# GpSimd's additions and reciprocal root moved in their steps, and PSUM additions given to VectorE in the second batch

## The chip, the cores and the metric

One core of one Trainium2 chip runs the whole program. The metric is device microseconds (us) of one execution, the median of several runs. A profiled execution is one further run, recorded by the hardware profiler; its engines are called PE (TensorE, with PEld for its weight loads), DVE (VectorE), ACT (ScalarE), POOL (GpSimd) and SP (the queue that issues most DMAs).

## What is computed

Inputs are q, k, v of shape (8 batches, 8 heads, 576 positions, 64) and two MLP weights, all float32. First comes attention in which each row keeps its 32 largest scores:

```python
scores = scale * np.matmul(q, k.transpose(0, 1, 3, 2))
kth = np.partition(scores, -top_k, axis=-1)[..., -top_k:-top_k + 1]
scores = np.where(scores >= kth, scores, -1000000000.0)
attn = np.exp(scores - np.max(scores, axis=-1, keepdims=True))
attn = attn / (np.sum(attn, axis=-1, keepdims=True) + 1e-09)
x = np.matmul(attn, v)          # heads side by side: x is (8, 576, 512)
```

Then Fourier mixing over positions and channels, a normalisation, and an MLP of width 2048:

```python
mixed = np.real(np.fft.fft(np.fft.fft(x, axis=1), axis=2))
u = x + mixed
un = (u - mean(u)) / np.sqrt(var(u) + 1e-06)      # over the 512 channels
out = u + np.maximum(un @ w_ch1, 0.0) @ w_ch2
```

## The kernel before

The attention is cut into 288 tiles of 128 query rows (36 to a batch). One pass of the main loop is a *step*: in step i VectorE searches the 32 largest scores of tile i (second half) and tile i+1 (first half). It is four rounds of MAX8 and three of MATCH_REPLACE8 on 128x576 scores (L446, L448, in `top_ops`). TensorE makes the scores of tile i+3 (`scores`, L392 to L425), into one of six score buffers S. After the search GpSimd forms the tile's bounds nt (L455, `bounds`), ScalarE the mask (L469), GpSimd subtracts it (L472), ScalarE takes the exponential (L480) and splits the words (L493); a DMA writes them to DRAM ("planes") and another brings them back transposed (PT), and TensorE multiplies by v a few steps later (L585, o). The result is transposed back (L626, tpx), and VectorE normalises it into the batch's x (L630). Two x buffers exist, so a batch writes its x only when the batch two before it has stored its own.

Behind the attention of a batch follow its Fourier section and its MLP, laid between the steps of the next batch's attention. The Fourier section: GpSimd folds x into sums and differences (L685, L696, L762, near), TensorE transforms along positions (L809, yp), ScalarE copies that out (L834 to L847, y and yt), TensorE transforms along channels (L860, L864, mp; `dft_channels`), and the result is added to x. Only row tiles 0, 1 and 4 are computed; tiles 3 and 2 get the mirrored channels of tiles 0 and 1. There are two ways to add it:

- `add_mixed` (batches 1 to 6; batches count from 0): ScalarE copies mp from PSUM to a tile us (L874), GpSimd adds it to x (L898), a step later VectorE takes the statistics.
- `add_at_once` (first and last batch): VectorE adds from PSUM directly (L880): four additions for tile 0 and its mirror, four for tile 1, one for tile 4, nine in all.

Then `stats` (L909, L910, VectorE) per row tile, `rsqrt` (variance to reciprocal root: three VectorE operations, then four Newton passes of four GpSimd operations each, L928 to L933), and `channels_first` (x transposed on TensorE, L948, and copied out by ScalarE, L951, unT). The MLP is a queue of *units*: 32 hidden units a batch (L1055, hp, relu on ScalarE, L1059), then units of the second product. That second product is plain for the first batch (`back`, L1082) and for the last two row tiles of batches 1 to 5, and in seven half-size products elsewhere (L1254, cv and cw). In `back`, ScalarE scales the finished product (L1108) and GpSimd adds it to x (L1110); for row tile 3, VectorE does both (L1096), a step later.

The order of the work is written by the program itself: `at(step, where, fn)` files a piece of work under a step and a place in it; `run(i, where)` plays it back. Units are taken from the queue between the fixed pieces of a step so that the TensorE cost per step, counted with fixed numbers (1.75 us for a unit of the second product), stays level until the next batch's units arrive (`arrivals`, `level`). All engines execute in that order. Places on GpSimd, in order within a step: mask subtraction, whatever the units issue, "pool0", sums for the seven products, the bounds nt, then "pool" and "pool2". On VectorE: search, late work, "dve", "stats". Stores are filed under "load2", last in the step, on SP's or GpSimd's queue.

Matmul results of this part go to three PSUM banks used in turn (`bank`). A bank may be held until its reader has been issued.

In the second batch (`soon`, b = 1), step 81 holds the channel transforms of row tiles 0 and 1, step 82 that of tile 4, steps 81 to 83 the additions, 82 to 84 the statistics, 84 the root, and its MLP units arrive at step 86.

Of the kernel before, what the change touches and what calls it, by code (L numbers as in the profile page):

```python
# [86 lines left out]
def kernel(  # L87
# [761 lines left out]
    def dft_channels(b, t, quick=False):  # L849

        rows, y = ROWS[t], y_of[b]
        shape, name = [P, 2, DM // 2], f"mp_{b}_{t}"
        mp = ps_s.tile(shape, F32, name=name, tag="sp") if b == B - 1 else bank(shape, name)
        def of(g):
            if t == 4:
                return yt_of[b][:, g].rearrange("p h r -> p (h r)")
            return y[:, g, t, :]

        for g in range(2):
            nc.tensor.matmul(  # L860
                mp[0:rows, 0, g:DM // 2:2], lhsT=of(g), rhs=fd[:, g], start=True, stop=True
            )
        for g in range(2, 4):
            nc.tensor.matmul(  # L864
                mp[0:rows, 1], lhsT=of(g), rhs=fd[:, 2 * g - 2:2 * g],
                start=(g == 2), stop=(g == 3),
            )
        if quick:
            at(now[0], "dve", lambda: add_at_once(b, t, mp))
            return 1.75  # L870
        if b not in us_of:
            us_of[b] = batp.tile([P, 3, DM], F32, name=f"us_{b}", tag="fold_s")
        us = us_of[b][0:rows, CHUNKS[0].index(t), :]
        nc.scalar.copy(out=two(us), in_=mp[0:rows])  # L874
        return 1.75
# [36 lines left out]
    def rsqrt(b):  # L912

        vr = small.tile([P, 5], F32, name=f"vr_{b}", tag="vr", bufs=2)
        gi = small.tile([P, 5], I32, name=f"gi_{b}", tag="gi", bufs=2)
        t2 = small.tile([P, 5], F32, name=f"t2_{b}", tag="t2", bufs=2)
        rs_of[b] = rs = gi.bitcast(F32)
        nc.vector.tensor_scalar(
            out=vr, in0=mv[b % 2][:, :, 1], scalar1=1e-6, scalar2=None, op0=ALU.add
        )  # L920
        nc.vector.tensor_scalar(
            out=gi, in0=vr.bitcast(I32), scalar1=1, scalar2=None, op0=ALU.arith_shift_right
        )
        nc.vector.tensor_scalar(
            out=gi, in0=gi, scalar1=-1, scalar2=0x5F3759DF, op0=ALU.mult, op1=ALU.add
        )
        for _ in range(4):
            nc.gpsimd.tensor_tensor(out=t2, in0=rs, in1=rs, op=ALU.mult)  # L928
            nc.gpsimd.tensor_tensor(out=t2, in0=t2, in1=vr, op=ALU.mult)
            nc.gpsimd.tensor_scalar(  # L930
                out=t2, in0=t2, scalar1=-0.5, scalar2=1.5, op0=ALU.mult, op1=ALU.add
            )
            nc.gpsimd.tensor_tensor(out=rs, in0=rs, in1=t2, op=ALU.mult)  # L933

    def channels_first(b, t):

# [104 lines left out]
    def mlp_units(b):  # L1041
# [33 lines left out]
        def back(ch, t, part):  # L1075
            n, hT, rs = CHUNKS[ch].index(t), hT_of[ch], rs_of[b]
            if part == 0:
                cps[t] = bank([P, DM], f"cp_{b}_{t}", True)
            cp, free = cps[t]
            if t != 4:  # L1080
                for it in range(2 * part, 2 * part + 2):
                    nc.tensor.matmul(  # L1082
                        cp, lhsT=hT[:, it, P * n:P * (n + 1)], rhs=w2[:, it, :],
                        start=(it == 0), stop=(it == NIT - 1),
                    )
                if part == 7:
                    xt = x[:, t, :]

                    def store():
                        store_rows(b, t)  # L1090
                        stored.append(t)
                        if len(stored) == 4:
                            written.add(b)

                    def finish():
                        nc.vector.scalar_tensor_tensor(  # L1096
                            out=xt, in0=cp, scalar=rs[:, t:t + 1], in1=xt, op0=ALU.mult, op1=ALU.add
                        )
                        free()

                    if last:
                        finish()
                    elif t == 3:

                        late_next.append(finish)
                    else:
                        ct = ct_of(t)
                        nc.scalar.mul(out=ct, in_=cp, mul=rs[:, t:t + 1])  # L1108
                        free()
                        nc.gpsimd.tensor_tensor(out=xt, in0=xt, in1=ct, op=ALU.add)  # L1110

                    if last:
                        store()
                    else:
                        at(now[0] + 2 + t % 2, "load2", store)
                return

            for it in range(2 * part, 2 * part + 2):
                for g in range(2):
                    nc.tensor.matmul(  # L1120
                        cp[TAIL * g:TAIL * (g + 1), :],
                        lhsT=hT[:, NIT // 2 * g + it, P * n:P * n + TAIL],
                        rhs=w2[:, NIT // 2 * g + it, :],
                        start=(it == 0), stop=(it == NIT // 2 - 1),
                    )
            if part == 3:
                tails_done(cp, free)
                if begins:
                    begins.pop()()
# [269 lines left out]
    def at(step, where, fn, cost=0.0):  # L1399
        plan.setdefault((step, where), []).append(fn)  # L1400
        costs[step] = costs.get(step, 0.0) + cost
# [92 lines left out]
    for b in range(B):  # L1494
        end = PER_BATCH * (b + 1) - 1
        last = b == B - 1
        first, soon = b == 0, b == 1
        T0 = end + (2 if first else 3 if soon or last else 5)
        for hp in range(NPB - 1):
            at((end - 4 + (0, 2, 3)[hp] if first else end + hp), "pool2", lambda b=b, hp=hp: fold_pair(b, nc.gpsimd, hp))  # L1500
        quick = first or last
        for n, op in enumerate(fold_tails(b, nc.gpsimd)):
            if quick:
                at(T0 - 2 if first else T0 - 1, "pool" if first else "pool0", op)
            else:
                at(T0 + n - (2 if soon else 1), "pool0", op)

        def folds(b=b, T0=T0, quick=quick, soon=soon, last=last):
            ops = fold_ops(b, nc.vector if quick else nc.gpsimd)
            for n, op in enumerate(ops):  # L1510
                if quick:
                    op()
                    if last and n == 0:
                        some_sums(1.3)
                else:
                    at(T0 + 1 + (min(n, 3) if soon else n), "pool0", op)

        at(T0, "dve" if quick else "begin", folds)
        if last:

            at(T0 + 1, "pe1", lambda: one_unit() + one_unit() if len(queue) > 1 else 0.0)
        ft, fc = {
            "first": ((T0 + 1, T0 + 1), T0 + 1), "last": ((T0 + 1, T0 + 2), T0 + 3),
            "soon": ((T0 + 6, T0 + 7), T0 + 7), "": ((T0 + 6, T0 + 8), T0 + 9),
        }["first" if first else "last" if last else "soon" if soon else ""]
        if first:
            at(ft[0], "pe1", lambda b=b: dft_tokens_both(b), 5.8)
        else:
            for par in range(2):
                at(ft[par], "pe1", lambda b=b, par=par: dft_tokens(b, par), 2.9)  # L1530
        for n, t in enumerate((0, 1, 4)):
            s = fc + (0 if quick else n // 2)
            at(s, "pe2", lambda b=b, t=t, q=quick: dft_channels(b, t, q), 1.75)
        for n, t in enumerate((0, 1, 4, 3, 2)):
            s = fc + (n // 3 if last else 0 if first else (0, 0, 1, 1, 2)[n])
            if quick:
                at(fc, "stats", lambda b=b, t=t: stats(b, t))
            else:
                at(s, "pool2", lambda b=b, t=t: add_mixed(b, t))
                at(s + 1, "dve", lambda b=b, t=t: stats(b, t))  # L1540
            at(s + (1 if quick else 2), "pe", lambda b=b, t=t: channels_first(b, t), 0.6)
            if first and t == 4:
                at(s + 1, "pe", lambda: (queue.extend(waiting), waiting.clear()) and 0.0)
        at(s + 1, "begin" if quick else "dve", lambda b=b: rsqrt(b))
        arrivals.append(s + (1 if quick else 3))
        at(arrivals[-1], "units", lambda b=b: (queue if b else waiting).extend(mlp_units(b)))

    queue, waiting, pending, written, now, out_next = [], [], [], set(), [0], []
# [261 lines left out]
```

## Time and profile before

| what | value |
|---|---|
| median of 3 runs | 1774.47 us (1772.94 to 1776.26) |
| profiled execution, its own time | 1769.09 us |
| its span, first to last instruction | 1767.3 us |
| busy: TensorE / VectorE / ScalarE / GpSimd | 92% / 88% / 72% / 51% of the span |
| mean granted TensorE clock | 0.968 of full |

A row of the timeline gives start, duration, engine, line, operation, output and input, and how many instructions were merged; in square brackets stands the idle time before it and what ended it. The columns of the stretches are busy time and instruction count of each engine, then TensorE's granted clock, the DMA engines' busy share and GB/s. In the groups of instructions the numbers behind the bar are busy time, mean ns of one, and idle time of the engine just before, with what ended most of it. A row of the waits gives the total, how many, and the longest.

### The profile page before, as it was taken

Reading aid. Unit: us, or ns where it says so; the run is one execution under the profiler, and the core shown is the slowest. Engines: PE = TensorE matmul, PEld = TensorE weight load, DVE = VectorE, ACT = ScalarE, POOL = GpSimd, SP = SyncE. Lnnn points to the kernel's source line nnn. Section 1 sums busy time; section 2 is a strip of 40 time slices with the busy share of each in tenths; the row PEclk is TensorE's granted clock in tenths of the full one; section 3 lists DMA queues with packets and bytes.
Section 4 is the critical chain, followed back from the end, with each engine's and each line's share of the span. In section 5 each row is a group of like instructions: output and inputs, shape, how many; then the busy total and the mean of one; then the engine's idle time right before and its main releaser. Section 6 shows DMA issues by size and latency. Waiting matters only on the chain.

```text
span 1767.3 us, 26298 instructions
## 1 busy us (share of the span) xinstructions
PE 1631.0 (92%) x7830; PEld 1044.8 (59%) x7830; DVE 1548.3 (88%) x3319; ACT 1278.2 (72%) x3136; POOL 907.0 (51%) x1269
## 2 busy tenths in 40 slices
PE   5666789999899999999999999999999999999999
PEld 2444455464465755666556755576566755678777
DVE  7999999999999999999899999999999999873121
ACT  6887769886888778877888778777877778653200
POOL 4667876656636465455544565366535555433000
PEclk8878889999999999999999999999999999999999
DMA  5333226661457855596557846585558645643151
GB/s 157 103 92 95 78 82 173 184 156 41 127 139 198 223 134 137 142 235 167 130 140 185 230 125 147 148 239 152 142 133 223 183 128 132 171 126 102 36 182 60
DMA packets 492926, 255.28 MB, mean 144 GB/s; under 512 B 364528, under 2 KB 483056, under 8 KB 492784
## 3 DMA queue, kind: packets, MB, share of 16 engines
q1 hardware_dynamic: 489008, 243.80, 52.0%
q0 software_dynamic: 2816, 9.44, 1.6%
q8 instruction: 63, 1.03, 0.2%
q14 instruction: 79, 0.65, 0.1%
q10 hardware_dynamic: 960, 0.36, 0.1%
HBM read 99.79 MB, written 84.74 MB: 104 GB/s over the span
## 4 chain that ended last, share of the span: by engine, by line
PE 51%; DVE 17%; ACT 15%; POOL 10%; issue 4%; DMA 2%; SPq 0%; POOLq 0%; DVEq 0%; ACTq 0%
PE hp L1055 20%; DVE m L446 8%; DVE wk L448 8%; PE o L585 7%; PE cw L1254 5%; PE cv L1254 4%; PE sp L422 4%; POOL wk L472 4%; ACT wk L469 3%; PE cp L1120 3%; POOL fold L696 3%; ACT S L425 2%; ACT wk L493 2%; PE tpP L548 1%; PE sp_t L392 1%
## 5 line engine op out<-in xcount | busy, mean ns | idle before, releaser
L472 POOL TENSOR_TENSOR wk<-S,wk 128x576 f32<-128x576 f32 x288 | 407.4, 1415 | 444.9 <-ACT wk L469 444.0
L446 DVE MAX8 m<-wk 128x8 f32<-128x576 f32 x864 | 618.2, 742 | 0.1
L1055 PE MATMUL hp<-unT,w 128*128 128x256 f32 (+1 forms) x2048 | 528.5, 409 | 11.0 <-ACT hT L1059 3.7
L1055 PEld LDWEIGHTS hp<-unT,w 128*128 128x128 f32 x2048 | 377.3, 191 | 116.9 <-ACT hT L1059 10.4
L448 DVE MATCH_REPLACE8 wk<-m,wk 128x576 f32<-128x576 f32 x576 | 425.6, 739 | 0.0
L493 ACT COPY wk<-S 128x576 uint16<-128x576 uint16 x468 | 290.7, 675 | 0.0
L469 ACT ACTIVATE wk<-S,nt 128x576 f32<-128x576 f32 x288 | 224.8, 780 | 89.5 <-POOL nt L455 88.7
L446 DVE MAX8 m<-S 128x8 f32<-128x576 f32 x288 | 214.9, 746 | 11.2 <-ACT S L396 10.5
L480 ACT ACTIVATE S<-wk,nt 128x576 f32<-128x576 f32 x234 | 185.5, 793 | 46.5 <-POOL wk L472 45.6
L448 DVE MATCH_REPLACE8 wk<-m,S 128x576 f32<-128x576 f32 x288 | 212.8, 739 | 0.3 <-issue 0.3
L1059 ACT ACTIVATE hT<-hp 128x320 f32<-128x320 f32 (+1 forms) x256 | 104.6, 413 | 140.2 <-PE hp L1055 135.1
L1082 PE MATMUL cp<-w,hT 128*128 128x512 f32 x448 | 205.5, 597 | 0.0
L585 PE MATMUL o<-PT,v 128*64 128x256 f32 (+3 forms) x1440 | 196.5, 417 | 6.3 <-DMA PT<-planes 3.9
L422 PE MATMUL sp<-kT,qT 64*128 64x512 f32 (+1 forms) x528 | 163.2, 660 | 7.1 <-ACT S L414 4.2
L585 PEld LDWEIGHTS o<-PT,v 128*64 128x64 f32 x1440 | 114.4, 154 | 82.1 <-issue 21.6
L425 ACT COPY S<-sp 128x512 f32<-128x512 f32 (+1 forms) x264 | 141.9, 590 | 28.3 <-PE sp L422 27.3
L455 POOL TENSOR_TENSOR nt<-m,cc 128x2 f32<-128x2 f32 x288 | 57.5, 200 | 167.5 <-DVE m L446 162.2
L1254 PE MATMUL cw<-w,hT 128*128 128x256 f32 x512 | 120.3, 385 | 7.5 <-ACT ct L1225 2.8
L1082 PEld LDWEIGHTS cp<-w,hT 128*128 128x128 f32 x448 | 80.7, 192 | 76.4 <-issue 76.0
L392 PEld LDWEIGHTS sp_t<-kt,qT 128*128 128x128 f32 x320 | 50.1, 192 | 107.3 <-issue 63.9
L1254 PEld LDWEIGHTS cw<-w,hT 128*128 128x128 f32 x512 | 96.2, 192 | 24.3 <-POOL hT L1198 4.2
L1254 PE MATMUL cv<-w,hT 128*128 128x256 f32 x432 | 99.4, 380 | 0.0
(156 smaller groups left out, 2038.9 us busy)
## 6 DMA issues: line engine op xcount, KB each, us to landing
planes<-wk SPq DMA_DIRECT2D x208, 288.0 KB, 2.6
w<-w_parts SPq DMA_DIRECT2D x94, 512.0 KB, 4.7
space<-in_moe_w_ch_dram SPq DMA_DIRECT2D x32, 512.0 KB, 3.4
nat<-in_q_dram SPq DMA_DIRECT2D x128, 64.0 KB, 2.3
v<-in_v_dram SPq DMA_DIRECT2D x32, 256.0 KB, 3.4
nat<-in_k_dram SPq DMA_DIRECT2D x62, 128.0 KB, 2.8
planes<-wk SPq DMA_DIRECT2D x52, 144.0 KB, 2.6
w_parts<-w_t POOLq DMA_DIRECT2D x8, 512.0 KB, 4.5
```

The lines of the kernel that those rows point to most:

```text
L422: nc.tensor.matmul(sp[r], lhsT=qT[hd, q_cols], rhs=kT[hd, :], start=True, stop=True)
L425: nc.scalar.copy(out=s_t[r, keys], in_=sp[r])
L446: ops.append(lambda src=src, m8=m8: nc.vector.max(out=m8, in_=src))
L448: ops.append(lambda src=src, m8=m8: nc.vector.match_replace(w, m8, src, NEG))
L469: nc.scalar.activation(out=w, in_=Ssb[i], func=AF.Relu, scale=-FAR, bias=Nt[i][:, 1:2])
L472: nc.gpsimd.tensor_tensor(out=w, in0=Ssb[i], in1=w, op=ALU.subtract)
L480: nc.scalar.activation(out=Ssb[i] if by_dma(i) else w, in_=w, func=AF.Exp, bias=Nt.pop(i)[:, 0:1], accum_out=den_t[pair % 3][:, c:c + 1],)
L493: nc.scalar.copy(out=words[:, half, :], in_=src[:, half, :])
L585: nc.tensor.matmul(o[D * e:D * (e + 1), c0:c1], lhsT=vv[:, e, c, :], rhs=pt[:, NF if c == NF else (NF + 1) * e + c, c0:c1], start=(c == 0) ...
L1055: nc.tensor.matmul(hp[:, 0:w], lhsT=w1[:, dt, P * it:P * (it + 1)], rhs=unT[:, dt, 0:w], start=(dt == 0), stop=(dt == NDT - 1),)
L1082: nc.tensor.matmul(cp, lhsT=hT[:, it, P * n:P * (n + 1)], rhs=w2[:, it, :], start=(it == 0), stop=(it == NIT - 1),)
L1254: nc.tensor.matmul(dst, lhsT=h()[a][:, kc, :], rhs=rhs_of(kc), start=start and kc == 0, stop=kc == NK - 1, skip_group_check=True,)
```

## The change

Three things, independent of each other in the code.

1. In `back`, GpSimd's addition of a finished row tile to x is no longer issued where the product's last unit stands but filed under "pool" of the same step, behind the bounds nt. It is eight additions: row tiles 0, 1 and 2 of the first batch, tile 2 of batches 1 to 5.
2. In `rsqrt`, the four Newton passes are filed under "pool" of four successive steps. The last batch keeps them together.
3. For the second batch, `dft_channels` takes the way of `add_at_once`: nine VectorE additions from PSUM at the end of the step that makes the product, statistics in that step, transposes, root and the arrival of the MLP's units one to two steps earlier (arrival at step 84). As the planner levels TensorE's cost up to each arrival, the first batch's units are packed a little closer (done in step 79 instead of 81), the second's a little wider, and at each later batch change one or two units stand a step later.

```diff
-        for _ in range(4):
+        def newton():
             nc.gpsimd.tensor_tensor(out=t2, in0=rs, in1=rs, op=ALU.mult)
             nc.gpsimd.tensor_tensor(out=t2, in0=t2, in1=vr, op=ALU.mult)
             nc.gpsimd.tensor_scalar(
                 out=t2, in0=t2, scalar1=-0.5, scalar2=1.5, op0=ALU.mult, op1=ALU.add
             )
             nc.gpsimd.tensor_tensor(out=rs, in0=rs, in1=t2, op=ALU.mult)
+        for n in range(4):
+            if b == B - 1:
+                newton()
+            else:
+                at(now[0] + n, "pool", newton)
...
                         nc.scalar.mul(out=ct, in_=cp, mul=rs[:, t:t + 1])
                         free()
-                        nc.gpsimd.tensor_tensor(out=xt, in0=xt, in1=ct, op=ALU.add)
+                        at(now[0], "pool", lambda: nc.gpsimd.tensor_tensor(
+                            out=xt, in0=xt, in1=ct, op=ALU.add
+                        ))
...
-            at(s, "pe2", lambda b=b, t=t, q=quick: dft_channels(b, t, q), 1.75)
+            at(s, "pe2", lambda b=b, t=t, q=quick or soon: dft_channels(b, t, q), 1.75)
         for n, t in enumerate((0, 1, 4, 3, 2)):
-            s = fc + (n // 3 if last else 0 if first else (0, 0, 1, 1, 2)[n])
+            s = fc + (n // 3 if last else 0 if first else (0, 0, 1, 1, 1 if soon else 2)[n])
             if quick:
                 at(fc, "stats", lambda b=b, t=t: stats(b, t))
+            elif soon:
+                at(s, "stats", lambda b=b, t=t: stats(b, t))
             else:
                 at(s, "pool2", lambda b=b, t=t: add_mixed(b, t))
                 at(s + 1, "dve", lambda b=b, t=t: stats(b, t))
-            at(s + (1 if quick else 2), "pe", lambda b=b, t=t: channels_first(b, t), 0.6)
+            at(s + (1 if quick or soon else 2), "pe", lambda b=b, t=t: channels_first(b, t), 0.6)
...
-        arrivals.append(s + (1 if quick else 3))
+        arrivals.append(s + (1 if quick else 2 if soon else 3))
```

## The prediction, made before the changed kernel ran

> **What bounds the kernel now.** I read the page's engine shares first, then busy time by stretches cut at the batches' own Fourier sections, then the timeline of each engine in the one stretch where two engines lose time at once.
>
> ```profile
> PE 1631.0 (92%) x7830; PEld 1044.8 (59%) x7830; DVE 1548.3 (88%) x3319; ACT 1278.2 (72%) x3136; POOL 907.0 (51%) x1269
> ```
> ```profile
> core 0: us, PE busy (x) PEld busy (x) DVE busy (x) ACT busy (x) POOL busy (x), PEclk, DMA share, GB/s
> 238.50:455.00 216.50, 204.57 (x886) 115.66 (x887) 213.51 (x456) 172.40 (x435) 139.39 (x198) 0.98 0.53 138
> 455.00:500.00 45.00, 37.76 (x222) 23.81 (x219) 38.15 (x86) 38.23 (x102) 24.30 (x41) 0.96 0.48 127
> 500.00:702.00 202.00, 190.23 (x909) 118.56 (x907) 197.82 (x423) 161.32 (x392) 106.02 (x155) 0.99 0.66 170
> 702.00:897.00 195.00, 190.84 (x920) 119.90 (x920) 186.20 (x400) 154.85 (x378) 103.73 (x153) 1.00 0.65 166
> ...
> 1285.00:1480.00 195.00, 191.14 (x920) 119.88 (x920) 185.79 (x399) 154.87 (x378) 103.62 (x153) 1.00 0.64 167
> ...
> 1595.00:1767.00 172.00, 167.29 (x796) 133.04 (x794) 41.25 (x89) 29.11 (x79) 20.57 (x46) 1.00 0.31 97
> ```
>
> Length less busy time is idle time. Up to 702 VectorE is the tighter engine: it idles 3.0 us of 216.5 and 4.2 us of 202, TensorE 11.9 and 11.8. From 702 on it is TensorE: 3.9 to 4.2 us idle in 195, VectorE 8.8 to 9.2. In the last 172 us only TensorE matters. The exception is 455 to 500, the second batch's Fourier section, where both idle about 7 us (7.2 and 6.9). That is where the third part of the change lies. VectorE and TensorE there:
>
> ```profile
> 456.11 0.75 DVE L446 MAX8 m<-S 128x8 f32<-128x576 f32 x1
> ...
> 460.93 0.75 DVE L446 MAX8 m<-S 128x8 f32<-128x576 f32 x1
> ...
> 465.88 0.74 DVE L1096 SCALAR_TENSOR_TENSOR x<-cp,gi,x 128x512 f32<-128x512 f32 x1
> 468.83 0.69 DVE L909 BATCH_NORM_STATS2 st<-x 128x6 f32<-128x512 f32 x1 [2.21 <-POOL x L898]
> ...
> 470.17 0.69 DVE L909 BATCH_NORM_STATS2 st<-x 128x6 f32<-128x512 f32 x1 [0.43 <-POOL x L898]
> ...
> 477.45 0.69 DVE L909 BATCH_NORM_STATS2 st<-x 128x6 f32<-128x512 f32 x1 [0.48 <-POOL x L898]
> ...
> 492.63 0.42 DVE L630 TENSOR_TENSOR x<-tpx,rd 128x256 f32<-128x256 f32 x1 [3.23 <-DMA out_dram<-x,out_list]
> ```
> ```profile
> 465.22 0.71 PE L860 MATMUL mp<-fd,y 128*128 128x128 f32 x4 [1.50 <-ACT yt L847]
> 465.76 1.03 PE L864 MATMUL mp<-fd,y 128*128 128x256 f32 x4
> ...
> 467.07 1.03 PE L864 MATMUL mp<-fd,y 128*128 128x256 f32 x4
> ...
> 476.09 0.46 PE L948 MATMUL tpu<-turns,x 64*128 64x64 f32 x4 [0.34 <-POOL x L898]
> 479.81 0.63 PE L948 MATMUL tpu<-turns,x 128*128 128x128 f32 x4 [3.26 <-ACT unT L951]
> 480.37 4.07 PE L585 MATMUL o<-PT,v 128*64 128x256 f32 x20
> ...
> 487.55 0.55 PE L626 MATMUL tpx<-turns,xT 128*128 128x128 f32 x3 [1.64 <-ACT xT L599]
> ...
> 488.37 2.32 PE L1055 MATMUL hp<-unT,w 128*128 128x320 f32 x8
> ```
>
> A VectorE step of search alone is 460.93 - 456.11 = 4.82 us. VectorE waits 2.21 + 0.43 + 0.48 us for GpSimd's additions of the channel results and 3.23 us for a store that frees the first batch's x. TensorE waits 1.50 + 0.34 + 3.26 + 1.64 = 6.74 us, and the first product of the second batch's MLP (hp) starts at 488.37.
>
> **The change, part by part.**
>
> *Third part: VectorE adds from PSUM, second batch only.* Nine additions go to VectorE, in the form that the first batch already runs. Three ScalarE copies and GpSimd's five tile additions go away; the statistics, the transposes and the MLP's start move one to two steps earlier (first hp in step 84 instead of 86).
>
> ```profile
> 240.56 3.32 DVE L880 TENSOR_TENSOR x<-mp,x 128x512 f32<-128x512 f32 x9
> ```
>
> So +3.32 us of VectorE work, on the engine that binds here. More matters where it stands: at the end of step 81, in front of step 82's search. Step 81's search ends at 460.93; L1096 moves ahead of it (the first batch's units end two steps earlier), so VectorE stands at the addition at 460.93 + 0.74 = 461.67. The first channel result ends at 465.76 + 1.03 = 466.79. The start of that product does not move up: it waits for ScalarE's copies (yt, 1.50 us), and this change takes nothing out of ScalarE ahead of them. VectorE therefore waits 466.79 - 461.67 = 5.12 us. The second result (467.07 + 1.03 = 468.10) is there when the first tile's four additions are done (about 468.3). Queued behind the wait are the statistics and step 82's search; behind those GpSimd's bounds, ScalarE's mask and TensorE's transposes of step 82. TensorE itself is not starved of scores, which it makes three steps ahead. Two of three PSUM banks are held until these additions; the third takes the tails' product.
>
> Against it: the three waits for GpSimd (3.12 us) go, their cause being removed. The 3.23 us wait goes too: that store stands on GpSimd's queue behind the reciprocal root,
>
> ```profile
> 484.68 0.20 POOL L928 TENSOR_TENSOR t<-gi 128x5 f32<-128x5 f32 x1 [1.46 <-DVE gi L924]
> ...
> 488.86 0.20 POOL L933 TENSOR_TENSOR gi<-gi,t 128x5 f32<-128x5 f32 x1
> 489.58 1.11 POOL L1031 DMA_INDIRECT out_dram<-x,out_list  x1 [0.52 <-issue]
> ```
>
> and afterwards it is issued in step 82, ahead of the root. Balance on VectorE at the start of step 86: +5.12 + 3.32 - 3.12 - 3.23 = **+2.1 us**. Bounds: +5.3 if the store wait is only exchanged for another, and -3.0 if TensorE's result came just when VectorE arrives.
>
> [...]
>
> *TensorE's load after it.* The second batch's units now fill steps 84 to 125 instead of 86 to 124, so each step of that batch carries less TensorE work. VectorE idles 4.2 us in that stretch (500 to 702), mostly in two waits:
>
> ```profile
> 591.56 0.42 DVE L630 TENSOR_TENSOR x<-tpx,rd 128x256 f32<-128x256 f32 x1 [2.05 <-PE tpx L626]
> ...
> 667.78 0.76 DVE L446 MAX8 m<-S 128x8 f32<-128x576 f32 x1 [1.30 <-ACT S L396]
> ```
>
> Between nothing and 4.2 us comes back; I take **-1.0**, half of the one wait that is for TensorE. At the batch change the old order ran out of units a step early and started the next batch with three; the new one starts with two. The third had to wait for the bank that VectorE's last addition frees:
>
> ```profile
> 702.15 2.42 PE L1055 MATMUL hp<-unT,w 128*128 128x320 f32 x8 [1.14 <-DVE x L1096]
> 897.08 2.42 PE L1055 MATMUL hp<-unT,w 128*128 128x320 f32 x8 [0.50 <-DVE x L1096]
> ...
> 1480.26 2.42 PE L1055 MATMUL hp<-unT,w 128*128 128x320 f32 x8 [0.55 <-DVE x L1096]
> ```
>
> Five such waits (702 to 1480). In the new order that bank comes up two steps later, long after it is free. The last four, 0.50 to 0.56 us each, lie where TensorE binds: **-2.1**. On the other side, in the middle of each later batch the new order is one or two units behind the old one at the same step. That costs nothing while TensorE is never out of work, and where it is, up to 3.5 us (two units at the planner's cost of 1.75 us).
>
> *Second part: the reciprocal root over four steps.* One stretch of 489.06 - 484.68 = 4.4 us on GpSimd becomes four of 1.1 us, each behind its step's bounds (nt). Its result is first read some 20 units later. What lies ahead of the next mask subtraction there is, on average, a wait anyway:
>
> ```profile
> L472 POOL TENSOR_TENSOR wk<-S,wk 128x576 f32<-128x576 f32 x288 | 407.4, 1415 | 444.9 <-ACT wk L469 444.0
> ```
>
> 444.9 / 288 = 1.5 us per step, more than 1.1. So the parts are covered; without that cover they would cost 3 x 1.1 us of GpSimd delay per batch. What goes is a delay of masks and of their transfers. From the third batch on two TensorE waits name the bounds, neither of them near a root (the roots stand just ahead of the batch changes at 702, 897 and so on):
>
> ```profile
> 974.60 3.69 PE L1254 MATMUL cw<-w,hT 128*128 128x256 f32 x16 [0.78 <-POOL nt L455]
> ...
> 1550.97 1.97 PE L1254 MATMUL cw<-w,hT 128*128 128x256 f32 x8 [1.53 <-POOL nt L455]
> ```
>
> I take 0; bounds 0 to -3 us per batch.
>
> *First part: GpSimd's MLP additions at the end of their step.* Eight additions (three of the first batch, one in each of five others).
>
> ```profile
> POOL x L1110 <- ACT hT L1108: 11.2, 6, 2.3
> ```
>
> GpSimd stood 11.2 / 6 = 1.9 us each before bounds that were ready. Now the bounds pass first and the addition falls into the same mask wait as above. Cost 0, gain 0 off the binding engines; bounds +0.5 and -1.9 each. The row store is two to three steps later and is not reached.
>
> **Sum.** +2.1 - 1.0 - 2.1 = -1.0 us on the profiled execution, whose own time is 1769.1 us (span 1767.3). That execution was faster than all three runs shown, median 1774.5, so I put the median after at 1774.5 - 1.0 = **1773.5 us**. A difference under 0.2% (3.5 us) is about what this measurement cannot tell from none.
>
> **Rivals.**
> *TensorE gains the whole section (faster).* If VectorE's wait is made up within its 4.2 us of later slack, what counts is TensorE: of its 6.74 us of waits all but the 1.50 for yt go, 5.2 us. The product behind them goes faster as well: 4.07 us at 480.37 against 2.38 for the same form here:
>
> ```profile
> 528.51 2.38 PE L585 MATMUL o<-PT,v 128*64 128x256 f32 x20 [0.59 <-PE hp L1055]
> ```
>
> That is 1.7 us more, and with the 2.1 of the bank waits -9.0: 1765.5 us. For it: 7.2 us of TensorE idle time in that section. Against: VectorE is the tighter engine before and behind it. [...]
> *The wait is carried to the end (slower).* One mechanism: VectorE's stall in step 81 (+5.1 and 3.3 of work) is not recovered before 702, and the third batch then starts two units behind, 3.5 us, which TensorE, binding from there, never makes up. +2.1 + 3.5 = +5.6: 1780 us. For it: VectorE has but 4.2 us slack up to 702. It decides if TensorE idles over 3 us more than before between 702 and 800.
> *GpSimd's root was on the path after all (faster).* If masks released 3 us earlier in each of the five later batches shorten them, TensorE's 3.9 to 4.2 us of idle time per batch caps it; half of that in five batches is -10: 1764.5 us. Against: none of those waits is for the mask's chain.
>
> **How the numbers follow.** Forecast 0.43, TensorE gains 0.22, carried to the end 0.28, root on the path 0.07. The forecast's own range is +-3.5 us (1770 to 1777) and counts as no change: same 0.43, faster 0.29, slower 0.28. The range 1764 to 1782 takes in all three rivals with two us beyond the slower one, whose +5.6 leaves the shift in DMA timing uncounted; both ends leave under 0.2.
>
> **What would show it.** Right: VectorE waits about 5 us for mp near 462; nine L880 additions there; no wait of L630 for the store; first hp about 480; none of the five bank waits; roots in four pieces; the time at the third batch's start within 2 us of before. Wrong: no wait for mp (TensorE was earlier), a batch of the later five longer or shorter than 194 to 195 by over 1 us, or new waits of TensorE for the sums of GpSimd (hT), whose places shift with the units.

## The result, and the profile after

The changed kernel takes 1760.28 us (median of 6 executions, 1758.32 to 1762.07), the kernel before on the same chip 1774.79 (6 executions, 1772.94 to 1776.26). The ratio is 0.9919, with a 95% interval of 0.9908 to 0.993: 14.5 us faster. The forecast was 1773.5, and its range ended at 1764.

The page of the changed kernel, busy time of each engine:

```profile
PE 1637.9 (93%) x7830; PEld 1052.2 (60%) x7830; DVE 1555.1 (88%) x3329; ACT 1280.8 (73%) x3133; POOL 898.4 (51%) x1261
```

TensorE has 7830 matmuls in both kernels, and VectorE ten instructions more after than before; what differs is where time is lost. To see where, I cut both traces at the same steps (a step's time is that of its bounds nt, L455) and read busy time by stretch. The columns are those of the prediction. First before: steps 58 to 79, 79 to 86, 86 to 126, and then one later batch, 234 to 270.

```profile
347.61:455.94 108.33, 100.01 (x461) 58.84 (x460) 105.61 (x223) 82.88 (x214) 67.05 (x102) 0.97 0.41 107
455.94:497.43 41.49, 34.25 (x198) 21.85 (x197) 34.74 (x78) 35.18 (x95) 21.76 (x40) 0.96 0.45 124
497.43:706.28 208.85, 196.93 (x941) 122.23 (x941) 204.56 (x438) 167.55 (x406) 109.63 (x160) 0.99 0.65 168
...
1289.30:1484.39 195.09, 191.15 (x924) 119.89 (x922) 185.88 (x399) 154.87 (x380) 103.71 (x153) 1.00 0.64 166
```

The same stretches after, and behind them the last one:

```profile
350.16:467.00 116.84, 108.14 (x482) 64.74 (x478) 105.68 (x223) 84.06 (x216) 66.50 (x100) 0.94 0.41 101
467.00:510.06 43.06, 35.05 (x191) 22.18 (x190) 40.78 (x93) 34.41 (x94) 14.40 (x28) 0.92 0.45 123
510.06:715.97 205.91, 196.57 (x940) 120.61 (x939) 204.78 (x437) 168.11 (x405) 108.99 (x156) 0.98 0.66 172
...
1285.55:1475.90 190.35, 189.08 (x920) 119.56 (x917) 185.65 (x399) 154.93 (x377) 103.56 (x153) 1.00 0.67 173
...
1585.08:1760.00 174.92, 170.34 (x812) 136.03 (x810) 41.57 (x90) 29.93 (x81) 19.06 (x45) 1.00 0.30 96
```

The second batch's Fourier section (79 to 86), about which most of the prediction turned, is 1.6 us longer and the stretch behind it 2.9 shorter. The end of the first batch (58 to 79) is 8.5 us *longer*. The gain is in the later batches: 195.09 to 190.35 in the one shown, 778.1 to 759.9 in the four from step 126 to 270, 18 us, at a granted clock of 1.00 in both. After, TensorE idles 1.3 us of 190.35 there; before it was 3.9 of 195.09. The last stretch is 2.9 us longer (172.03 before).

The profiled execution of before (1769.09) lies 5.7 us under its median and that of after (1762.07) is the slowest of its six, so the two traces differ by only 7, and a stretch set against before's trace shows less than the whole gain. Therefore traces are read here for *where*, medians for *how much*.

### The profile page after: what moved, and what is told of

It is laid out like the page before. It is cut to its first block, busy times and chain, and to the rows that moved or that the text cites. A ratio compares the mean times of both kernels' runs of the same rounds, so it can differ in the third digit from the quotient of the medians.

```text
span 1760.3 us, 26272 instructions
## 1 busy us (share of the span) xinstructions
PE 1637.9 (93%) x7830; PEld 1052.2 (60%) x7830; DVE 1555.1 (88%) x3329; ACT 1280.8 (73%) x3133; POOL 898.4 (51%) x1261
## 4 chain that ended last, share of the span: by engine, by line
PE 54%; DVE 7%; POOL 4%; ACT 4%; issue 2%; DMA 1%; SPq 0%; POOLq 0%; DVEq 0%
PE hp L1062 20%; PE cw L1263 6%; PE o L585 5%; PE cv L1263 5%; PE cp L1089 4%; PE sp L422 4%; DVE m L446 3%; DVE wk L448 3%; PE cp L1129 3%; PE sp_t L392 2%; POOL wk L472 1%; POOL fold L696 1%; PE yp L809 1%; ACT wk L469 1%; PE mp L864 1%
## 5 line engine op out<-in xcount | busy, mean ns | idle before, releaser
L1062 PEld LDWEIGHTS hp<-unT,w 128*128 128x128 f32 x2048 | 382.2, 192 | 114.4 <-issue 9.0
L455 POOL TENSOR_TENSOR nt<-m,cc 128x2 f32<-128x2 f32 x288 | 57.7, 200 | 197.7 <-DVE m L446 194.9
```

Source lines behind the costliest of these rows:

```text
L1062: nc.tensor.matmul(hp[:, 0:w], lhsT=w1[:, dt, P * it:P * (it + 1)], rhs=unT[:, dt, 0:w], start=(dt == 0), stop=(dt == NDT - 1),)
```

## Experiments

Lengths of the stretches in the profiled executions (us), by steps, for the kernels that follow:

| kernel | 58-79 | 79-86 | 86-126 | 126-270 | 270-287 | median |
|---|---|---|---|---|---|---|
| before | 108.3 | 41.5 | 208.8 | 778.1 | 110.6 | 1775 to 1778 |
| after | 116.8 | 43.1 | 205.9 | 759.9 | 109.2 | 1760.28 |
| e1, part 1 | 108.5 | 41.5 | 210.8 | 769.5 | 110.8 | 1761.57 |
| e2, part 2 | 108.6 | 40.1 | 208.0 | 779.2 | 110.6 | 1773.57 |
| e3, part 3 | 119.4 | 43.3 | 206.1 | 764.8 | 110.2 | 1770.84 |
| e4, parts 1, 2 | 107.3 | 40.1 | 208.6 | 769.1 | 110.8 | 1759.38 |
| e5, places alone | 108.4 | 41.5 | 210.0 | 768.0 | 110.2 | 1766.30 |
| e8, part 2 + places | 108.7 | 40.0 | 208.6 | 766.9 | 108.3 | 1758.39 |
| e9, part 1 + places | 108.6 | 41.5 | 210.5 | 761.3 | 110.7 | 1754.92 |
| e7, parts 1, 2 + places | 107.4 | 39.9 | 208.2 | 760.5 | 109.2 | 1751.07 |
| e6, after, old places | 117.1 | 42.9 | 205.9 | 771.7 | 110.8 | 1771.85 |
| e10, after, old packing | 107.2 | 44.5 | 205.7 | 759.3 | 109.4 | 1751.38 |
| e11, part 1, later batches only | 108.2 | 41.5 | 208.5 | 772.7 | 110.8 | 1764.60 |
| e12, the same, ahead of nt | 108.3 | 41.5 | 208.9 | 777.4 | 110.6 | 1770.53 |

"Packing" means how closely the first batch's units stand up to step 81. "Places" means the steps at which the units of the third and all later batches stand. The third part shifts them as a side effect, since the planner's account of TensorE time (`carry`) arrives at the third batch with 0 instead of -2.64.

### Each part alone: e1, e2, e3, and parts 1 and 2: e4

e1_adds has only the diff's second hunk (the addition filed under "pool"), e2_root only the first (`newton`), e3_psum only the third, e4_adds_root the first two:

```diff
-                        nc.gpsimd.tensor_tensor(out=xt, in0=xt, in1=ct, op=ALU.add)
+                        at(now[0], "pool", lambda: nc.gpsimd.tensor_tensor(
+                            out=xt, in0=xt, in1=ct, op=ALU.add
+                        ))
```

> The kernel before with the first part alone: GpSimd's eight MLP additions at the end of their step. Whoever holds that the gain comes from the reciprocal root, or from the order of the units behind the second batch, expects 1773 to 1776 us (no change). If GpSimd's wait in front of bounds that were ready was on the path, each of the five later batches gets 1 to 2 us shorter: 1765 to 1770 us.

> The kernel before with the second part alone: four Newton passes over four steps. Theory A (the root blocked masks that TensorE's work of the later batches needed): the five later batches shrink from 194 to 195 us to 190 to 191 each, 1757 to 1763 us in all. Theory B (the gain is the order of the MLP units behind the second batch): 1772 to 1776 us.

> The kernel before with the third part alone: VectorE adds from PSUM in the second batch, and the planner starts each later batch with two units instead of three. Theory A: the section costs or saves 2 us and nothing follows, 1772 to 1778 us. Theory B: the later batches shrink by 3 to 4 us each, 1758 to 1764 us.

> First and second part, every unit of the MLP where it stood before, no third part. It closes the table. If the third part's loss with unshifted units (1772 us with all three parts) is the denser packing of the first batch and nothing else, this stands about 9 us lower than that run, 1759 to 1764 us. If the root has a gain of its own beside the first part, it stands 3 us or more below the first part alone (1762 us).

Measured: e1 1761.57 against 1775.09 (ratio 0.9917, 0.9885 to 0.995); e2 1773.57 (0.9991, 0.9976 to 1.0006); e3 1770.84 (0.998, 0.9966 to 0.9994); e4 1759.38 against 1777.69 (0.9898, 0.987 to 0.9926). The first part, which I had costed at nothing, is worth some 13.5 us by itself (9 to 20 by its interval), and lies below even the 1765 to 1770 us that were expected if GpSimd's wait was on the path. The root alone is nothing that this can tell from none, as forecast. The third part alone, with the places and the packing that it brings, gains 4, between the two ranges expected. e4 lies 2 us below e1, less than the 3 us that were to show a gain of the root.

Why, shows GpSimd's timeline in the one step per batch where the addition of the finished row tile falls. Before:

```profile
1432.86 1.41 POOL L472 TENSOR_TENSOR wk<-S,wk 128x576 f32<-128x576 f32 x1 [1.13 <-ACT wk L469]
1435.94 1.27 POOL L1110 TENSOR_TENSOR x<-x,hT 128x512 f32<-128x512 f32 x1 [1.67 <-ACT hT L1108]
1437.17 2.14 POOL L762 TENSOR_TENSOR near<-fold 128x513 f32<-128x513 f32 x2
1439.27 0.19 POOL L455 TENSOR_TENSOR nt<-m,cc 128x2 f32<-128x2 f32 x1
```

In e1, the same step:

```profile
1428.47 1.42 POOL L472 TENSOR_TENSOR wk<-S,wk 128x576 f32<-128x576 f32 x1 [1.12 <-ACT wk L469]
1429.84 2.15 POOL L762 TENSOR_TENSOR near<-fold 128x513 f32<-128x513 f32 x2
1431.93 0.21 POOL L455 TENSOR_TENSOR nt<-m,cc 128x2 f32<-128x2 f32 x1
1432.07 1.30 POOL L1110 TENSOR_TENSOR x<-x,hT 128x512 f32<-128x512 f32 x1
```

Behind the addition stood not only the bounds but the fold's last piece, near, and it is this step in which TensorE begins the Fourier section with near. The addition's wait and the addition, 1.67 + 1.27 = 2.94 us, came ahead of both. Who waited for them before (TensorE, ScalarE, VectorE):

```profile
1438.31 0.47 PE L809 MATMUL yp<-fs,near 128*64 128x145 f32 x4 [0.46 <-POOL near L762]
...
1442.10 1.89 PE L422 MATMUL sp<-kT,qT 64*128 64x512 f32 x4 [0.58 <-ACT S L414]
```
```profile
1439.49 0.78 ACT L469 ACTIVATE wk<-S,nt 128x576 f32<-128x576 f32 x1 [3.63 <-POOL nt L455]
```
```profile
1443.94 0.19 DVE L612 RECIPROCAL rd<-rd 128x6 f32<-128x6 f32 x1 [1.75 <-ACT rd L611]
...
1445.88 0.76 DVE L446 MAX8 m<-S 128x8 f32<-128x576 f32 x1 [1.74 <-ACT S L396]
```

In e1 neither TensorE wait stands there, ScalarE and VectorE wait 0.7 and 0.63 us:

```profile
1432.17 0.78 ACT L469 ACTIVATE wk<-S,nt 128x576 f32<-128x576 f32 x1 [0.70 <-POOL nt L455]
```
```profile
1438.55 0.76 DVE L446 MAX8 m<-S 128x8 f32<-128x576 f32 x1 [0.63 <-ACT S L396]
```

So one late GpSimd result passes through ScalarE (a wait of 3.63 us), whose copies of the scores stand behind the mask (mask at 1439.49, first copy at 1441.31), to VectorE (1.75 and 1.74 us) and TensorE (0.46 and 0.58 us). The time of the bounds against before moves by -2.95 us at exactly this step (153, 189, 225, 261) in each of four batches, and at steps 116 to 117 by -2.1. That sums to 13.9 us. Not all of it lasts: by the next such step -2.2 to -2.4 of the -2.95 are left, and the batches in the table are 1.7 to 2.4 us shorter.

### Which additions, and past what: e11 and e12

```diff
+                        def add():
+                            nc.gpsimd.tensor_tensor(out=xt, in0=xt, in1=ct, op=ALU.add)
+                        if b:
+                            at(now[0], "pool", add)
+                        else:
+                            add()
```

e11_adds_later moves only the additions of batches 1 to 5, one each. e12_adds_pool0 is the same with "pool0" for "pool": behind near, still ahead of the bounds.

> The first part for the additions behind the first batch alone (one in each of five batches); the first batch's three stay where they were. If the addition that stands in front of the fold's last operations (near) and of the bounds is the cause, this keeps the whole gain of the first part: 1759 to 1766 us. If the first batch's additions made it: 1772 to 1777 us.

> As the run before, but the addition is put behind the fold's last operations (near) and still in front of the bounds nt. So near is released 2.9 us earlier and the bounds are as late as before. If the fold's chain into the Fourier section is what was late: the same gain, 1759 to 1766 us. If it is the bounds (mask, then ScalarE's copies of scores queued behind it): 1771 to 1777 us.

e11: 1764.6 against 1777.79 (0.993, 0.9906 to 0.9955), 13.2 us: five instructions carry the first part, and the first batch's three do little. e12: 1770.53 (0.9954, 0.9936 to 0.9972), 7.3 us. e11 lies in the range expected if these additions are the cause; e12 lies between its two ranges. By steps e12's bounds move by -1.7 us at the four places and -1.0 at step 116, 7.9 in all. By these medians passing near is worth somewhat more than half, and passing the bounds too the rest (13.2 - 7.3 = 5.9); the intervals of e11 and e12 overlap, so the split is not shown as firmly as the sum.

In e12's profiled execution the later batches are nevertheless hardly shorter than before's (777.4 against 778.1). What is won at these steps is lost again before the next of them, at places where the program is unchanged. TensorE in one batch, before and then e12:

```profile
1351.27 2.38 PE L585 MATMUL o<-PT,v 128*64 128x256 f32 x20 [0.57 <-DMA PT<-planes]
...
1363.12 1.10 PE L1254 MATMUL cw<-w,hT 128*128 128x256 f32 x4 [0.54 <-ACT kT L339]
```
```profile
1353.21 2.38 PE L585 MATMUL o<-PT,v 128*64 128x256 f32 x20 [1.41 <-DMA PT<-planes]
...
1365.52 1.97 PE L1260 MATMUL cw<-w,hT 128*128 128x256 f32 x8 [1.00 <-DMA w<-w_parts]
```

The waits of e12 are for transfers, of the transposed masks and of the MLP's weights. They vary between batches and kernels: where TensorE waits for the weights in e1, e11 and e12, it is for 1.0 to 2.5 us. In the changed kernel the trace names a transfer for no TensorE wait over 0.3 us from step 90 to 287.

### The shifted places: e5, e8, e9, e7

e5_phase is before with the changed kernel's later places; e8_root_phase has the root in addition, e9_adds_phase the additions, e7_adds_root_phase both (all but the third part):

```diff
         if i in arrivals:
             carry = min(carry, 0.0) if i > arrivals[0] else -5.0
+            if i == arrivals[2]:
+                carry = 0.0
```

> The kernel before, nothing of the change in it, but the planner's carry set to 0 instead of -2.64 where the third batch's units arrive, so that from there on every unit stands in the step where the changed kernel has it. Theory A (root): 1772 to 1777 us. Theory B (order of the units): the later batches shrink by 3 to 4 us each, 1757 to 1763 us. If both are needed together, between these.

> The kernel before with the second part and the shifted units, without the first part. Theory C says that with the units shifted the addition no longer stands in front of the fold, so the first part has nothing left to do, while the root in one piece costs 2.4 us at each batch change (a wait of TensorE for ScalarE there): within 2 us of the run with all of it but the third part, 1751 to 1759 us. If the first part has a gain of its own: 1760 to 1766 us, as with the shifted units alone.

> First part and the shifted units, without the second part. If the root in one piece costs nothing once the rest is done: 1750 to 1754 us, as with root and all. If it costs what the runs with and without it differed by behind shifted units alone (about 8 us): 1757 to 1761 us.

> First and second part, and the planner's carry set to 0 where the third batch's units arrive, without the third part: VectorE does not add from PSUM in the second batch and the first batch's units are packed as before. Theory C: the later batches as short as in the changed kernel (189 to 190.5 us each) and the stretch from step 58 to 79 back at 108 us from 117: 1750 to 1757 us. If the third part itself saves time: 1760 us or more.

e5: 1766.3 against 1775.09 (0.9944, 0.9922 to 0.9967). e8: 1758.39 against 1776.85 (0.9901, 0.9884 to 0.9917). e9: 1754.92 against 1777.79 (0.9871, 0.9846 to 0.9896). e7: 1751.07 against 1776.85 (0.9857, 0.9841 to 0.9874), the fastest of all.

Of what was expected of these, e7 came as its first theory said; e5 and e9 lie between their two ranges. e8's 1758.39 is in the range of the theory that the first part has nothing left to do beside shifted places, but e7, which is e8 with the first part added, is 7 us faster: that theory is out.

So places alone give 9 us, and beside the first part still 7 (1761.57 to 1754.92). What they remove is seen between e1 and e9. TensorE in one later batch of e1, all its waits over 0.4 us:

```profile
1346.44 2.38 PE L585 MATMUL o<-PT,v 128*64 128x256 f32 x20 [0.74 <-DMA PT<-planes]
1358.75 1.97 PE L1256 MATMUL cw<-w,hT 128*128 128x256 f32 x8 [1.00 <-DMA w<-w_parts]
1374.82 1.99 PE L1055 MATMUL hp<-unT,w 128*128 128x256 f32 x8 [0.56 <-ACT hT L1059]
1377.29 1.99 PE L1055 MATMUL hp<-unT,w 128*128 128x256 f32 x8 [0.47 <-ACT hT L1059]
```

Before has the last two as well, 0.52 and 0.47 us. And in the changed kernel, the same batch:

```profile
1361.41 1.97 PE L1263 MATMUL cw<-w,hT 128*128 128x256 f32 x8 [0.61 <-issue]
1443.03 0.51 PE L809 MATMUL yp<-fs,near 128*128 128x144 f32 x2 [0.62 <-ACT hT L1115]
```

With units standing one or two steps later, the weights, the transposed masks and the relus they read are there in time: these two waits are the only ones of TensorE in that batch. e9's batch has the same two waits of 0.61 and 0.62 us as the changed kernel, and one of 0.79 us at its end.

The two gains nearly add up. Per later batch (mean of four) before is 194.5 us, e1 192.4, e5 192.0, and e9 190.3: -2.1 and -2.5 alone, -4.2 together; by medians 13.5 and 8.8 alone, 22.9 together. TensorE's idle time in these batches of e9 is then 0.8 to 2.1 us, but for the first with 3.7. e5 also shows that its shift merely moves the addition's block: the addition then stands, with a wait of 2.39 us, ahead of the bounds two steps later,

```profile
1445.27 1.27 POOL L1110 TENSOR_TENSOR x<-x,hT 128x512 f32<-128x512 f32 x1 [2.39 <-ACT hT L1108]
1446.49 0.19 POOL L455 TENSOR_TENSOR nt<-m,cc 128x2 f32<-128x2 f32 x1
```

and gives 2.2 of the 2.95 us back there.

The root is worth 8 us beside the places (e5 to e8, 1766.3 to 1758.39), 4 beside additions and places (e9 to e7, 1754.92 to 1751.07) and 2 beside the additions (e1 to e4, 1761.57 to 1759.38); the last two are within what the intervals leave open. Between e5 and e8, and between e9 and e7, the table shows 1.5 us of it in the section 79-86, where the store's wait of 3.2 us gives way to one of 1.6 to 1.8 for transposes (e7, e2), 1.5 to 2.3 in 86-126, 1.5 to 2 in 270-287 and about 1 in the later batches.

Two things go some way to say why it is worth more in company than alone. Of the 10 us between the traces of e5 and e8, 3.9 lie in steps 0 to 36, in front of every difference of the two programs, and are not the root's. And in one piece the root does hold up a mask and, behind it, ScalarE for 3 to 4 us at each batch change: before at 1480.59, where TensorE's queue has no wait for it, and e5 at 1476.59.

```profile
1480.59 0.78 ACT L480 ACTIVATE S<-wk,nt 128x576 f32<-128x576 f32 x1 [4.05 <-POOL wk L472]
```
```profile
1476.59 0.78 ACT L480 ACTIVATE S<-wk,nt 128x576 f32<-128x576 f32 x1 [3.60 <-POOL wk L472]
```

In the shifted places TensorE waits for a relu that stands behind this on ScalarE's queue, at the last of these changes alone. e5, and then e8 with the root in four pieces:

```profile
1479.64 2.42 PE L1055 MATMUL hp<-unT,w 128*128 128x320 f32 x8 [2.42 <-ACT hT L1059]
```
```profile
1469.61 2.42 PE L1062 MATMUL hp<-unT,w 128*128 128x320 f32 x8 [0.22 <-ACT hT L1066]
```

How the rest of the 8 us divides was not separated.

### What the third part itself is worth: e6 and e10

e6_all_oldphase is the changed kernel with the later batches' old places (`carry = -2.64` in the edit above). e10_after_firstlevel is the changed kernel with the first batch's units packed as before:

```diff
             step_us = level(i)
+            if i == arrivals[0]:
+                step_us = 4.46
```

> The changed kernel with the planner's carry put back to -2.64 where the third batch's units arrive: all three parts, but from there on every unit in the step of the kernel before. Theory B (the gain of the later batches comes from the units' place): those batches go back to 194 to 195 us, 1772 to 1778 us in all. Theory C (the addition in front of the fold is what costs, and the first part or the shifted units each take it away): the batches stay at 191 to 193 us, 1762 to 1769 us.

> The changed kernel with one number: the first batch's units are taken at the old level (4.46 instead of 4.56 by the planner's count), so that they stand where they stood before, done in step 81. If the denser packing is what makes steps 58 to 79 longer (108 to 117 us), that stretch goes back to 108 to 110 us and the time to 1750 to 1756 us. If the third part itself did it, 1758 to 1763 us.

e6: 1771.85 against 1776.85 (0.9969, 0.9956 to 0.9982). Against e4, which lacks only the third part and its packing, that is 12 us slower: with old places, these two lose. Its total is next to what the theory of places gave, but its later batches (771.7 / 4 = 192.9 us) are as short as the other theory had them; what is lost is the stretch 58 to 79, 117.1 us against e4's 107.3. e10: 1751.38 (0.9864, 0.9847 to 0.988), 9 us faster than the changed kernel and equal to e7 (1751.07), which has no third part; both lie in the ranges expected if the packing alone costs. So the third part as such is worth nothing that this can tell, and the packing costs 9 us. The stretch 58 to 79 shows it, 116.84 after and 107.25 in e10. VectorE's waits over 0.5 us in that stretch of the changed kernel:

```profile
377.10 0.76 DVE L446 MAX8 m<-S 128x8 f32<-128x576 f32 x1 [0.77 <-ACT S L396]
395.69 0.76 DVE L446 MAX8 m<-S 128x8 f32<-128x576 f32 x1 [3.98 <-ACT S L396]
438.22 0.18 DVE L612 RECIPROCAL rd<-rd 128x4 f32<-128x4 f32 x1 [3.58 <-ACT rd L611]
441.12 0.42 DVE L630 TENSOR_TENSOR x<-tpx,rd 128x256 f32<-128x256 f32 x1 [2.73 <-PE tpx L626]
```

And of e10, its only one:

```profile
428.51 0.42 DVE L630 TENSOR_TENSOR x<-tpx,rd 128x256 f32<-128x256 f32 x1 [1.70 <-PE tpx L626]
```

That is 11.1 us against 1.7: the MLP's units, finished two steps earlier, crowd scores and transposes of a stretch in which VectorE has 2.7 us to spare (108.33 - 105.61).

TensorE is not idler there: 8.7 us after (116.84 - 108.14), 8.3 before. Its busy time grew by 8.1 us, for 482 records against 461 and at a granted clock of 0.94 against 0.97; in e10 it is 99.86 us at 0.98. In all 13.6 us of the changed kernel's stretch ran at half the clock (0.50 granted) and 6.8 of before's; in e10's, one product of eight matmuls (hp, 128x256) took 3.14 us at 377.01, the next 1.89 at 381.52. Two of the changed kernel's pieces:

```profile
386.10:393.00 6.90, 6.71 (x16) 4.35 (x17) 5.61 (x13) 3.23 (x7) 4.60 (x9) 0.51 0.39 86
433.90:437.30 3.40, 3.40 (x19) 2.69 (x14) 0.73 (x3) 0.59 (x2) 1.93 (x6) 0.50 0.00 0
```

VectorE's wait of 3.98 us begins in the first (391.71), that of 3.58 us in the second (434.64). So part of the 9 us is likely the slower clock; what the closer units take and what the clock takes was not separated, nor why the clock fell.

## Why the prediction was wrong

**The first part, "Cost 0, gain 0 off the binding engines": this step failed.** The idle time was read right for the six waits quoted (1.9 us each; two more of the eight, 4.7 us together, stand under another tile's name), and its bound ("-1.9 each") was per addition. But the gain was put at nothing because GpSimd does not bind, without asking who waits behind the addition; the mean mask wait of 1.5 us per step answers for the cost alone. The bounds and near stand behind the addition on the same queue, and one such step makes ScalarE wait 3.63 us, VectorE 1.75 and 1.74, TensorE 0.46 and 0.58. All these rows were in the trace of before. I also counted only the wait, not the addition (1.27 us) that had to be done first. The runs showed 2.95 us in place of nothing at each of four steps and 2.1 at a fifth, 13.5 us in all by e1's median, 13.2 of it by five additions alone (e11); my whole forecast was -1.0.

**The units' places: right that they change, wrong in size.** I costed five bank waits (-2.1) and named up to 3.5 us against. The bank waits are gone, and the last stretch is 2.9 us longer, as allowed for. But e5 gains 9, e9 another 7 on top of the first part: the waits for weights, transposed masks and relus, about 3 us in the batch of e1 that is shown, had no term in the sum. The row of cw with 0.78 us "for nt", which I quoted, was read as a wait for the bounds; in e12 the wait at the same place names the weights' transfer:

```profile
976.95 3.81 PE L1260 MATMUL cw<-w,hT 128*128 128x256 f32 x16 [1.27 <-DMA w<-w_parts]
```

That it was this transfer before too is likely, not shown; a GpSimd sum into hT ended at 974.42 there, just ahead as well.

**The third part: right in its waits, near in its sum partly by luck.** +2.1 was forecast at the start of step 86, 1.6 measured (e3 1.8, e10 3.0). VectorE waits for mp as described: with the third part alone (e3) 4.53 us for the 5.12 forecast, in the changed kernel 1.92, and with the old packing (e10) 2.56.

```profile
479.59 2.74 DVE L880 TENSOR_TENSOR x<-mp,x 128x512 f32<-128x512 f32 x8 [4.53 <-PE mp L864]
```
```profile
477.86 2.74 DVE L880 TENSOR_TENSOR x<-mp,x 128x512 f32<-128x512 f32 x8 [1.92 <-PE mp L864]
```
```profile
465.24 2.75 DVE L880 TENSOR_TENSOR x<-mp,x 128x512 f32<-128x512 f32 x8 [2.56 <-PE mp L864]
```

In e3 the terms come out: 4.53 in place of 5.12 gives +1.5, and 1.8 was measured. In the changed kernel they don't: with 1.92 the sum would be -1.1, yet 1.6 was measured. VectorE's busy time in the stretch is 6.0 us longer (34.74 to 40.78) where 3.3 were forecast for the additions; the nine additions and six further instructions, all of them search that lay outside the cut before, make it up. The wait for the store is gone in the changed kernel; in e10, whose section ran at a granted clock of 0.88 against 0.96, 0.83 us of it is left:

```profile
494.02 0.42 DVE L630 TENSOR_TENSOR x<-tpx,rd 128x256 f32<-128x256 f32 x1 [0.83 <-DMA out_dram<-x,out_list]
```

The first hp comes 24.0 us behind step 79's bounds (491.01 - 467.00; forecast 480 - 455.94 = 24). The recovery behind it was -2.9 instead of -1.0. What failed is a sentence of the change's description that I did not price: that the first batch's units "are packed a little closer". It cost 9 us. With it the sign "the third batch's start within 2 us of before" failed too: step 126 is 9.7 us later (715.97 against 706.28), 8.5 of them from the stretch 58 to 79 and 3.8 from steps 0 to 36, where the programs are the same.

**The root, 0: right alone** (e2), not in company (2 to 8 us by the medians). I looked for TensorE's waits near a root and found none; ScalarE stood 4 us behind it at each batch change already in the trace of before, and in the shifted places TensorE once stood behind ScalarE, for 2.42 us.

**The rivals.** "TensorE gains the whole section" is out: the section is 1.6 us longer, not 5.2 shorter. The 1.7 us that it gave for the product behind the waits are no gain either: TensorE is busy for 35.05 us in the section, 34.25 before. In the trace of before that product's 4.07 us lie at a granted clock of 0.58, the 2.38 us of the same form at 528.51 at 1.00; what lowers the clock was not shown. In the changed kernel this form takes 2.38 us at 495.80 (clock 1.00), but the first hp 3.74 us at 491.01 (0.63), against 2.32 at 488.37 before (1.00). "Carried to the end" is out: 86 to 126 is shorter. "Root on the path" has nearly the right time (1764.5), but by chance: it was for the wrong instruction, and the root alone gives nothing (e2). Its cap, TensorE's 3.9 to 4.2 us of idle time per later batch, was about the gain: 18.2 / 4 = 4.5 us per batch, of which in the batch shown 2.6 are idle time (3.9 to 1.3) and the rest shorter busy time. So it was no strict cap. I had it and the right stretch, and gave the mechanism 0.07 because I asked it of the root only. The sign by which the prediction named itself wrong, later batches shorter than 194 by over 1 us, is the one that came.

## What to carry to other kernels

For every instruction that a change moves, list what stands behind it on its engine's queue in the very step where it falls, and who needs that next; a mean over all steps hides one bad step per period, and here five instructions were worth 13 us. Where a planner places other work by a running account, a local edit moves work far away: price those shifts (here -9 us for the later batches' places and +9 for the first batch's packing) before the edit itself (the third part, about 0). And where an engine is 98% busy, its idle time in one period tells roughly what a reordering can give (here 3.9 us idle in the batch shown, 4.7 gained, as busy time shrank too); look which waits make it up, transfers among them.

## What the runs showed that was not expected

- **A wait won can be lost to a transfer.** In the batch shown of e1 and e12 TensorE waits 1.0 us for weights and 0.7 to 1.4 us for transposed masks, at steps where nothing was changed; before it was 0.54 and 0.57 us at the same places.
- **TensorE's busy time fell with its gaps.** The same batch shows 191.15 us busy for 924 matmul records before and 189.08 for 920 after. Part is the scores' product behind a wait, 1.89 us for four matmuls before (1442.10) and in e1 1.13 us:

```profile
1436.55 1.13 PE L422 MATMUL sp<-kT,qT 64*128 64x512 f32 x4
```

  They are two pairs of 1.12 us each in both. In e1 both pairs start at 1436.55 and run side by side; before, the second starts 0.77 us after the first, at 1442.87. The rest was not traced.
- **The fastest kernel had the least spread.** Executions of before ran from 1771.59 to 1780.16 us (20 of them), those of e7 from 1750.79 to 1751.43, but these are only four.
- **A stretch without any change still differs.** Steps 0 to 36 took 204.7 us in the profiled execution of before and 208.6 in that of after, 204.6 to 208.6 over all kernels, at granted clocks from 0.75 to 0.80 that do not order them (0.80 before, 0.79 after).
